# Twelve chunk-1 projection groups moved from the load phase into the segment loop of a recurrent-memory attention kernel, with the whole first V half ahead of the first softmax sums

## Chip, cores, metric

One core of a Trainium2 chip. The metric is the device time of one execution in microseconds (us), as the median of several executions. "Span" is the time from the first to the last instruction in a profiled execution; it is shorter than the device time (858.1 against 859.79 us in before). A ratio of two kernels is the mean time of one kernel's fast runs over the mean of the other's fast runs of the same rounds, so it is not quite the ratio of the medians that are quoted beside it.

Terms: to "evict" is to copy a result out of a PSUM bank, where PE leaves it; "PV" is the product p @ v; "landing" is the moment when a transfer's data have arrived; "issue" as the cause of a wait means that PE waited for nothing that the profile's semaphores show; "residue" is the segment number modulo four.

## The reference, cut to what matters

```python
mem = mem0                                     # 8 memory rows
for s in range(64):                            # 64 segments of 32 rows, one after the other
    h = concatenate([mem, x[32*s : 32*s+32]])  # 40 rows x 512
    q, k, v = h @ Wq, h @ Wk, h @ Wv           # 32 heads of 128
    p = softmax(mask(q @ k.T * scale))
    o = (p @ v) @ Wo
    mem = o[:8]                                # the next segment needs this
    outs.append(o[8:])
h = x + concatenate(outs)
# then a gMLP on layernorm(h): two projections, a 2048x2048 mix, an output projection
```

The memory makes the segments a chain. In the kernel each segment takes the 8 memory rows and the first 24 new rows in the chain itself. The last 8 new rows of each segment ("x rows") are projected apart, for 16 segments (a "chunk") at a time, since they do not depend on the memory.

## The kernel before

One program per engine; the order on PE (TensorE) is what the source says. Three phases: the load phase (16 MB of weights come in, chunk 0 and chunk 1 of the x rows are projected), the loop of 64 segments, and the gMLP tail.

The load phase projects both chunks completely. `start_group` does 16 matmuls into a PSUM bank and evicts it; `load_wo` fetches a quarter of Wo (1 MB); `load_vx(s)` fetches the projected V of the x rows for segment s, which went through DRAM (`vext_d`).

```python
    for n in range(8):                   # V of chunk 0, first half of V of chunk 1
        ...
        start_v(0, n)
        if n % 2 == 1:
            start_v(1, n // 2)
        ...                              # load_wo(0) at n == 4
    load_wo(1)
    for j in range(2):
        load_vx(j)
    for i in range(8, 12):               # K side, both chunks
        for ck in range(2):
            start_group(qkx_mm, qkx_evac, ck, i)
    for n in range(4, 8):                # second half of V of chunk 1
        start_v(1, n)
        if n % 2 == 1:
            load_wo(n // 2)
    for i in range(12, 16):
        for ck in range(2):
            start_group(qkx_mm, qkx_evac, ck, i)
```

Chunks 2 and 3 (48 groups) are projected inside the loop as filler, two quarters of a group ahead of PV and two behind it. One segment in four takes none after segment 12 (`xs = ... if gx and (j4 != 1 or s < 3 * DC)`); other filler (`wq`) is the Wo product of the x rows, eight pieces in four segments.

```python
        S_half(s, 0)                     # scores of heads 0..15
        sm_exp(0)                        # ACT
        for dc in range(3):
            V_half(s, 0, (0, 4), dc)     # three quarters of the first V half
        sm_sums(0)                       # needs the exponential
        sm_ln(0)
        S_half(s, 1)
        sm_exp(1)
        sm_rcp(0)
        V_half(s, 0, (0, 4), 3)
        V_evac(0, "dve")
        V_half(s, 1, (0, 2), 3, 3, 0, held=True)   # held: weights stay, no load
        V_half(s, 1, (2, 4), 3, 3, 1, held=True)
        V_half(s, 1, (0, 2), 2, 3, 0)
        V_half(s, 1, (2, 4), 2, 3, 1, held=True)
        sm_norm(0)
        sm_sums(1)
        ...                              # four more half-width V pieces, evictions
        fill(nw1)
        for f in xs[:2]: f()
        PV_half(s, 0)
        PV_half(s, 1)
        for f in xs[2:4]: f()
        fill(nw2)
        ...                              # eight evictions of PV
        Wo(WOQ, OB, 0, OC)               # needs all four quarters of Wo
        ...
        fill(nw4)
```

The softmax here doesn't subtract the row's maximum and nothing guards it: scores larger than these inputs give would overflow.

Of the kernel before, what the change touches and what calls it, by code (L numbers as in the profile page):

```python
# [178 lines left out]
def fast_path(nc, st, keep, A_x, A_mem0, A_Wq, A_Wk, A_Wv, A_Wo, A_seg_len, B_w_in, B_w_sp, B_b_sp, B_w_out, out):  # L179
# [7 lines left out]
    NSEG = S // SEG  # L187
    RB = S // 128
    DC = D // 128
# [205 lines left out]
    def ln_apply(j):  # L395
        t, tok = xbuf(j)
        k = j % 3
        dve(lambda e: e.tensor_scalar(out=t, in0=t, scalar1=mv1[:, k, 0:1], scalar2=rs1[:, k:k + 1], op0=ALU.subtract, op1=ALU.mult),
            reads=tok + [("mv1", k), ("rs1", k)], writes=tok)
# [102 lines left out]
    def vx_evac(ck, n, bank, eng="act"):  # L502
        if ck == 1 and n < 4:
            t, tok = (hbuf, xo)[n // 2][:, n % 2, :], [(("h", "xo")[n // 2], n % 2)]
        elif ck == 1:
            t = (Vs, V_sb)[n // 2 - 2][:, n % 2, :]
            tok = [("Vs", n % 2)] if n < 6 else [("V", n % 2, g) for g in range(4)]
        elif ck == 0:
            t, tok = part[:, n, :], [("part", n, 0), ("part", n, 1)]
        else:  # L510
            t, tok = Vs[:, 0, :], [("Vs", 0)]
        if eng == "act":
            act(lambda e: e.activation(out=t, in_=ps[:, bank, :], func=ACT.Copy, scale=VSC), reads=[PB(bank)], writes=tok)
        else:
            dve(lambda e: e.tensor_scalar(out=t, in0=ps[:, bank, :], scalar1=VSC, scalar2=None, op0=ALU.mult), reads=[PB(bank)], writes=tok)
        dst = vext_d[ck, n // 4, 2 * (n % 4):2 * (n % 4) + 2, :, :].rearrange("g p f -> p g f")
        sp(lambda e: e.dma_start(dst, t.rearrange("p (g f) -> p g f", g=2)), reads=tok, writes=[("vext", ck, n)])
# [24 lines left out]
    def QK(s, k, dc, first=0, last=3, held=False):  # L542
        b, p0, np_, mi, bank = QKP[k]
        sl = slot(s)
        ws = (w_q, w_k)[mi]
        h0, nh = 16 * b + 2 * p0, 2 * np_
        for c in range(4):
            rhs = ws[:, dc, :].rearrange("p (h c i) -> p c h i", c=4, i=32)[:, c, h0:h0 + nh, :]
            pe(lambda e, c=c, rhs=rhs: mm(e, held, ps[32 * c:32 * c + 32, bank, 0:32 * nh], hT[:, sl, dc, :], rhs,
                                          dc == first, dc == last, (0, 32 * c)),  # L550
               reads=[("hTx", (s // 4) % 3), ("hTm", s, dc // 2), ("W", mi, 2 * b), ("W", mi, 2 * b + 1)], writes=[PB(bank)])
# [60 lines left out]
    def sm_sums(b):  # L612
        bank = UBK[b]
        for c in range(4):
            q = slice(32 * c, 32 * c + 32)
            pe(lambda e, q=q, c=c: e.matmul(ps[q, bank, 224:384], lhsT=ones[:, q], rhs=E_sb[:, b, 0:160], start=True, stop=False,  # L616
                                            skip_group_check=True, tile_position=(0, 32 * c)),
               reads=[("E", b), "ones"], writes=[PB(bank)])
        for c in range(4):
            q = slice(32 * c, 32 * c + 32)  # L620
            pe(lambda e, q=q, c=c: mm(e, True, ps[q, bank, 224:384].rearrange("p (g q) -> p g q", q=40)[:, :, 0:16], ones[:, q],
                                      E_sb[:, b, 160:224].rearrange("p (g q) -> p g q", q=16), False, True, (0, 32 * c)),
               reads=[("Ex", b), "ones"], writes=[PB(bank)])
# [18 lines left out]
    def V_half(s, b, gs, dc, first=0, last=3, held=False):  # L642
        bank = VB[b, gs[0]]
        sl = slot(s)
        w = 128 * (gs[1] - gs[0])
        for c in range(4):
            c0 = (16 * b + 4 * c + gs[0]) * DH
            pe(lambda e, c=c, c0=c0: mm(e, held, ps[32 * c:32 * c + 32, bank, 0:w], hT[:, sl, dc, :], w_v[:, dc, c0:c0 + w],
                                        dc == first, dc == last, (0, 32 * c)),
               reads=[("hTx", (s // 4) % 3), ("hTm", s, dc // 2), ("W", 2, 2 * b), ("W", 2, 2 * b + 1)], writes=[PB(bank)])  # L650

    def V_evac(b, eng, gs=(0, 4)):
        bank = VB[b, gs[0]]
        dst, src = V_sb[:, b, 128 * gs[0]:128 * gs[1]], ps[:, bank, 0:128 * (gs[1] - gs[0])]
        tok = [("V", b, g) for g in range(*gs)]
        if eng == "act":
            act(lambda e: e.activation(out=dst, in_=src, func=ACT.Copy, scale=VSC), reads=[PB(bank)], writes=tok)
        else:
            dve(lambda e: e.tensor_scalar(out=dst, in0=src, scalar1=VSC, scalar2=None, op0=ALU.mult), reads=[PB(bank)], writes=tok)  # L659
# [85 lines left out]
    def load_h(rb):  # L745
        sp(lambda e: e.dma_start(hbuf[:, rb % 2, :], xr[:, rb, :]), writes=[("h", rb % 2)])
# [77 lines left out]
    def load_wo(hq):  # L824
        sp(lambda e, hq=hq: e.dma_start(w_o[:, 8 * hq:8 * hq + 8, :], wor[:, 8 * hq:8 * hq + 8, :]), writes=[("Wo", hq)])
        em.mark_const(("Wo", hq))
# [4 lines left out]
    def start_group(mm, ev, *a):  # L831
        cnt = scnt[0]
        scnt[0] += 1
        bk = ebank[cnt % 4]
        mm(*a, bk)
        ev(*a, bk, "act" if cnt % 2 == 0 else "dve")

    def start_v(ck, n):
        start_group(vx_mm, vx_evac, ck, n)
# [25 lines left out]
    load_wo(1)  # L865
    for j in range(2):
        load_vx(j)
    for i in range(8, 12):
        for ck in range(2):
            start_group(qkx_mm, qkx_evac, ck, i)  # L870
    for n in range(4, 8):
        start_v(1, n)
        if n % 2 == 1:
            load_wo(n // 2)
    for i in range(12, 16):
        for ck in range(2):
            start_group(qkx_mm, qkx_evac, ck, i)


    gx = []  # L880
# [4 lines left out]
    def vx_group(ck, n):  # L885
        gx.append([lambda dc=dc: vx_mm(ck, n, XB, dc) for dc in range(DC)] + [lambda: vx_evac(ck, n, XB, "dve")])

    for ck in (2, 3):
        for n in range(8):
            vx_group(ck, n)  # L890
        for r in range(4):
            for mi in range(2):
                for b in range(2):
                    qkx_group(ck, mi, r, b)

# [18 lines left out]
    for s in range(NSEG):  # L914
        j4 = s % 4
        rb = s // 4
        if j4 == 1 and rb > 0:
            load_h(rb - 1)
        if s == NSEG - 1:
            load_h(rb)  # L920
        if s % 2 == 1 and s // 2 < NWT:
            wT_piece(s // 2)
        if j4 == 0 and 2 <= rb + 2 < RB:
# [6 lines left out]
        if s > 0:  # L930
            mem_out(s - 1, 1)
            for f in late:
                f()
        QK(s, 0, 1)
        QK(s, 1, 1, last=2, held=True)
        QK(s, 0, 2)
# [25 lines left out]
            mask_pe()  # L962
        S_half(s, 0)
        sm_exp(0)
        for dc in range(3):
            V_half(s, 0, (0, 4), dc)
        sm_sums(0)
        sm_ln(0)
        S_half(s, 1)
        lastop["s"] = em.by_eng["pe"][-1]  # L970
        sm_exp(1)
        sm_rcp(0)
        V_half(s, 0, (0, 4), 3)
        V_evac(0, "dve")
        if s == NSEG - 1:
            sp(lambda e: e.dma_start(w_in1, winr[:, :, 0:FH]), writes=["w_in1"], after=[lastop["s"], lastop["x"]])
            sp(lambda e: e.dma_start(bsp_b, bass.AP(B_b_sp.tensor, B_b_sp.offset, [[0, 128], [1, S]])), writes=["bsp"], after=[lastop["k"]])
            for r in range(8, RB - 2):
                xn2T_dma(r, [lastop["s"], lastop["x"]])
        V_half(s, 1, (0, 2), 3, 3, 0, held=True)  # L980
        V_half(s, 1, (2, 4), 3, 3, 1, held=True)
        V_half(s, 1, (0, 2), 2, 3, 0)
        V_half(s, 1, (2, 4), 2, 3, 1, held=True)
        sm_norm(0)
        sm_sums(1)
        sm_ln(1)
        sm_rcp(1)
        V_half(s, 1, (0, 2), 1, 3, 0)
        V_half(s, 1, (0, 2), 0, 3, 0)
        V_half(s, 1, (2, 4), 0, 3, 1, held=True)  # L990
        V_half(s, 1, (2, 4), 1, 3, 1)
        lastop["v"] = em.by_eng["pe"][-1]
        V_evac(1, "dve", (0, 2))
# [4 lines left out]
            lastop["x"] = em.by_eng["pool"][-1]  # L998
            lastop["x"] = em.by_eng["pool"][-1]
        late = []  # L1000
        xs = gx.pop(0) if gx and (j4 != 1 or s < 3 * DC) else []
        if xs:
            nw1, nw2, nw4 = (2 if s < 3 * DC and j4 < 2 else 1), 0, (2 if s < 3 * DC and j4 != 2 else 1)
        else:
            nw1, nw2, nw4 = 3, 2, 1

        def fill(n):
            for f in wq[:n]:
# [37 lines left out]
            late.append(lambda: ln_stats(7))  # L1046
        if s == 3:
            late.append(lambda: (ln_apply(7), x_flip(7, RB, hTe[:, 0, :, :], [("hTe", 0, 0), ("hTe", 0, 1)])))
        if j4 == 1 and rb >= 2:
            late.append(lambda rb=rb: (xn2_apply(rb - 2, rb % 2), xn2_store(rb - 2, rb % 2)))  # L1050
        if j4 == 1 and rb > 0:
            assert not wq
            late.append(lambda rb=rb: WoX_evac(rb - 1))
            wq.append(lambda rb=rb: F_group(rb - 1, WXB))
            wq.append(lambda rb=rb: WoX_scatter(rb - 1, WXB))
            nw4 = 0
        if j4 == 2 and rb > 0:
            late.append(lambda rb=rb: F_add(rb - 1, WXB))
        if j4 == 3 and rb > 0:
            late.append(lambda rb=rb: h_done(rb - 1))  # L1060
        if s + 1 < NSEG:
            if j4 == 3:
                assert not wq
                wq.extend(lambda rb=rb, k=k: WoX_mm(rb, k // 2, range(4 * (k % 2), 4 * (k % 2) + 4)) for k in range(8))
            fill(nw4)
            assert not wq or j4 != 2
        else:
            for f in late:
                f()
        if s + 2 < NSEG:  # L1070
# [964 lines left out]
```

## Time and profile before

| | before |
|---|---|
| median of three runs | 861.03 us (859.86 to 861.23) |
| span of the profiled run | 858.1 us |
| granted TensorE clock | 1.0 |
| first exponential (loop has begun 4 us before) | 56.85 us |
| segments 1 to 11, mean | 9.91 us |
| segments 12 to 62, mean | 9.75 us |
| after the last first-half exponential | 183.8 us |

Segments are measured from one start of the first-half exponential on ACT to the next; the segment numbers in this text are those. From the page of before: busy time by engine, and the chain of work that ended last.

```profile
span 858.1 us, 45452 instructions
PE 844.5 (98%) x22504; PEld 426.0 (50%) x18920; DVE 506.2 (59%) x1312; ACT 471.3 (55%) x1359; POOL 156.1 (18%) x423
...
PE 94%; DMA 3%; DVE 1%; SPq 1%; issue 0%; ACT 0%
```

PE is the bound, but "98% busy" is not "98% at work", as this trace shows. The timeline of before in a middle segment, where the columns are start, duration, engine, line, instruction and operands:

```profile
254.52 0.82 PE L289 MATMUL f_ps<-f_arena,f_hT 128*32 128x512 bf16 x12
255.35 0.25 PE L616 MATMUL f_ps<-f_E_sb,f_ones 128*32 128x160 bf16 x4
...
256.83 0.39 PE L752 MATMUL f_ps<-f_arena,f_cTx 128*32 128x512 bf16 x4
257.04 0.60 PE L289 MATMUL f_ps<-f_arena,f_hTe 128*32 128x512 bf16 x8
257.58 0.20 PE L667 MATMUL f_ps<-f_E_sb,f_V_sb 32*128 32x40 bf16 x4
```

Four column-tiled 128x512 matmuls ("one quad") take 0.217 us (by their starts, nine in 1.95 us from 52.79 us on). Twelve take 0.65; but the first sums (L616) start 0.83 us after the twelve V matmuls began: 0.18 us of stall that no busy figure shows. The same before PV (L667): 0.54 us for two quads, which take 0.43.

Segment 0 of before:

```profile
59.48 0.27 PE L290 MATMUL f_ps<-f_arena,f_hT 128*32 128x256 bf16 x1 [0.69 <-issue]
...
61.10 0.51 PE L702 MATMUL f_ps<-f_arena,f_cT 128*32 128x256 bf16 x11
61.99 1.48 PE L702 MATMUL f_ps<-f_arena,f_cT 128*32 128x256 bf16 x45 [0.37 <-DMA f_arena<-in_A_Wo_dram]
```

What to see: the Wo product (L702) of segment 0 is stopped after 11 of its matmuls until the last quarter of Wo has landed (61.94 us in the landing records). So already before the change, Wo came just in time, though the loop began at 52.8 us.

### The profile page before, as it was taken

To read this page: it belongs to the slowest core of one execution; us is meant where nothing else is said; L and a number is where in the kernel's file an instruction comes from. 1 tells how busy PE (TensorE), PEld (TensorE's weight loads), DVE (VectorE), ACT (ScalarE), POOL (GpSimd) and SP (SyncE) were. 2 spreads that over 40 slices of the span, in tenths; PEclk is the share of its full clock that TensorE was granted. 3 is DMA by queue.
4 is the path that set the end of the run, shared out by engine and by line. 5 is a ranking of instruction groups with operands and counts; after the bars stand their busy time and mean duration, and the time that the engine had idled before them with its cause. 6 is when DMAs were issued, how large, how long until landed. Compare 5 with 4: busy or idle time off the path is not lost.

```text
span 858.1 us, 45452 instructions
## 1 busy us (share of the span) xinstructions
PE 844.5 (98%) x22504; PEld 426.0 (50%) x18920; DVE 506.2 (59%) x1312; ACT 471.3 (55%) x1359; POOL 156.1 (18%) x423
## 2 busy tenths in 40 slices
PE   8999999999999999999999999999999999999997
PEld 8664545444444544454444444444444444444443
DVE  3546666666666666666666666666665554453443
ACT  3446666666666666666666666666666655400000
POOL 0712112121112112121211212121111132100000
PEclk9999999999999999999999999999999999999999
DMA  9982222224141221222241413343121690032101
GB/s 315 365 256 68 72 76 70 66 40 86 31 87 41 70 46 51 72 68 60 71 86 38 80 43 94 69 83 71 47 69 43 193 277 1 1 111 98 38 13 41
DMA packets 114713, 75.25 MB, mean 88 GB/s; under 512 B 70728, under 2 KB 100560, under 8 KB 114512
## 3 DMA queue, kind: packets, MB, share of 16 engines
q1 hardware_dynamic: 114224, 72.06, 30.7%
q8 instruction: 164, 2.69, 1.3%
q14 instruction: 37, 0.30, 0.1%
q10 hardware_dynamic: 288, 0.20, 0.1%
HBM read 39.46 MB, written 20.58 MB: 70 GB/s over the span
## 4 chain that ended last, share of the span: by engine, by line
PE 94%; DMA 3%; DVE 1%; SPq 1%; issue 0%; ACT 0%
PE f_ps L289 30%; PE f_ps L702 13%; PE f_ps L290 13%; PE f_ps L1150 11%; PE f_ps L752 3%; PE f_ps L498 3%; PE f_ps L1224 3%; PE f_ps L667 3%; PE f_ps L1112 3%; PE f_ps L616 3%; PE f_ps L1143 3%; PE f_ps L463 2%; PE f_ps L596 1%; DMA f_arena<-in_A_Wq_dram 1%; DMA f_arena<-in_A_Wo_dram 1%; PE f_ps L673 1%
## 5 line engine op out<-in xcount | busy, mean ns | idle before, releaser
L289 PE MATMUL f_ps<-f_arena,f_hT 128*32 128x512 bf16 (+1 forms) x5120 | 352.4, 337 | 1.1
L290 PE MATMUL f_ps<-f_arena,f_hT 128*32 128x256 bf16 (+1 forms) x3072 | 214.0, 308 | 0.7 <-issue 0.7
L289 PEld LDWEIGHTS f_ps<-f_arena,f_hT 128*32 128x32 bf16 x5120 | 120.0, 96 | 170.0 <-issue 86.7
L560 ACT ACTIVATE f_Tst<-f_ps 128x512 bf16<-128x512 f32 (+1 forms) x320 | 149.7, 509 | 56.9 <-PE f_ps L289 53.3
L702 PE MATMUL f_ps<-f_arena,f_cT 128*32 128x256 bf16 x4096 | 130.4, 274 | 1.9 <-ACT f_cT L687 1.1
L639 POOL TENSOR_TENSOR f_E_sb<-f_R_sb,f_E_sb 128x64 bf16<-128x64 f32 x128 | 47.8, 374 | 373.1 <-ACT f_R_sb L631 373.1
L568 DVE STREAM_TRANSPOSE f_QT<-f_Tst 128x256 uint32<-128x256 uint32 x128 | 57.1, 446 | 94.5 <-ACT f_Tst L560 94.5
L702 PEld LDWEIGHTS f_ps<-f_arena,f_cT 128*32 128x32 bf16 x4096 | 89.9, 94 | 36.0 <-ACT f_cT L687 23.1
L1150 PE MATMUL f_ps<-f_arena 128*128 128x512 bf16 x448 | 100.6, 379 | 0.0
L659 DVE TENSOR_SCALAR f_V_sb<-f_ps 128x512 bf16<-128x512 f32 (+1 forms) x128 | 70.5, 551 | 41.5 <-PE f_ps L289 41.0
L689 DVE TENSOR_SCALAR f_cT<-f_ps 128x160 bf16<-128x160 f32 x256 | 65.0, 316 | 36.0 <-PE f_ps L673 36.0
L714 ACT ACTIVATE f_part<-f_ps 128x256 bf16<-128x256 f32 x128 | 49.0, 383 | 59.8 <-PE f_ps L702 56.8
L687 ACT ACTIVATE f_cT<-f_ps 128x160 bf16<-128x160 f32 x256 | 57.1, 310 | 36.8 <-PE f_ps L673 36.8
L1150 PEld LDWEIGHTS f_ps<-f_arena 128*128 128x128 bf16 x448 | 43.7, 98 | 52.8
L568 DVE STREAM_TRANSPOSE f_KT<-f_Tst 128x128 uint32<-128x128 uint32 (+1 forms) x192 | 65.9, 356 | 2.8
L627 ACT ACTIVATE f_R_sb<-f_ps 128x160 f32<-128x160 f32 x128 | 38.8, 304 | 33.7 <-PE f_ps L290 33.7
L1156 DVE TENSOR_TENSOR f_arena<-f_ps,f_arena 128x512 f32<-128x512 f32 x28 | 19.3, 689 | 54.4 <-PE f_ps L1150 52.4
L609 ACT ACTIVATE f_E_sb<-f_ps 128x224 bf16<-128x224 f32 x128 | 45.9, 359 | 0.0
L635 DVE TENSOR_TENSOR f_E_sb<-f_R_sb,f_E_sb 128x160 bf16<-128x160 f32 x128 | 44.7, 349 | 0.0
L631 ACT ACTIVATE f_R_sb<-f_R_sb 128x160 f32<-128x160 f32 x128 | 42.5, 332 | 2.0
L752 PE MATMUL f_ps<-f_arena,f_cTx 128*32 128x512 bf16 x512 | 40.6, 380 | 0.0
L289 PE MATMUL f_ps<-f_arena,f_hTe 128*32 128x512 bf16 x512 | 39.1, 382 | 0.0
(119 smaller groups left out, 1022.3 us busy)
## 6 DMA issues: line engine op xcount, KB each, us to landing
wT_d<-f_wst SPq DMA_DIRECT2D x32, 256.0 KB, 3.7
f_arena<-wT_d SPq DMA_DIRECT2D x32, 256.0 KB, 4.7
f_arena<-in_A_Wv_dram SPq DMA_DIRECT2D x4, 1024.0 KB
f_arena<-in_A_Wk_dram SPq DMA_DIRECT2D x4, 1024.0 KB, 16.1
f_arena<-in_A_Wo_dram SPq DMA_DIRECT2D x4, 1024.0 KB
f_Vx<-vext_d SPq DMA_DIRECT2D x128, 32.0 KB
f_arena<-in_A_Wq_dram SPq DMA_DIRECT2D x3, 1024.0 KB
vext_d<-f_Vs SPq DMA_DIRECT2D x18, 128.0 KB
```

Source lines behind the costliest of these rows:

```text
L289: return e.matmul(out, lhsT=lhsT, rhs=rhs, start=start, stop=stop, skip_group_check=True, tile_position=pos)
L290: return e.add_instruction(mybir.InstMatmult(name=nc.get_next_instruction_name(), engine=mybir.EngineType.PE, ins=[e.lower_ap(rhs), e.lowe ...
L560: act(lambda e: e.activation(out=st_.rearrange("p (hp i r) -> p hp i r", i=32, r=2), in_=ps[:, bank, 0:64 * np_].rearrange("p (hp r i) -> ...
L568: dve(lambda e: e.transpose(out=dst, in_=src), reads=tok, writes=[(nm, b, k) for k in halves(b, p0, np_)])
L639: pool(lambda e: e.tensor_tensor(out=ev, in0=rv, in1=ev, op=ALU.mult), reads=[("R", b), ("Ex", b)], writes=[("Ex", b)])
L659: dve(lambda e: e.tensor_scalar(out=dst, in0=src, scalar1=VSC, scalar2=None, op0=ALU.mult), reads=[PB(bank)], writes=tok)
L687: act(lambda e: e.activation(out=dst, in_=src, func=ACT.Copy, scale=UNSC), reads=[PB(PVB[c])], writes=tok)
L689: dve(lambda e: e.tensor_scalar(out=dst, in0=src, scalar1=UNSC, scalar2=None, op0=ALU.mult), reads=[PB(PVB[c])], writes=tok)
L702: pe(lambda e, h=h, g=g, i=i, b=b, c=c: e.matmul(ps[32 * g:32 * g + 32, bank, 0:d1 - d0], lhsT=cTh[:, i, 8:40], rhs=w_o[:, h, d0:d1], star ...
L714: act(lambda e: e.activation(out=part[:, s % 8, d0:d1], in_=ps[:, bank, 0:d1 - d0], func=ACT.Copy), reads=[PB(bank)], writes=[("part", s % ...
L752: pe(lambda e, h=h, g=g, i=8 * qr + bg: e.matmul(ps[32 * g:32 * g + 32, WXB, :], lhsT=cTx[:, rb % 2, i, :], rhs=w_o[:, h, :], start=(i < 4 ...
L1150: pe(lambda e: e.matmul(ps[:, bank, 0:TB], lhsT=z2[:, sc, fb * 128:(fb + 1) * 128], rhs=wTb[tb % 2][:, :, sc, :], start=(sc == 0), stop=(s ...
```

## The change

The intent: take 12 of the 24 chunk-1 groups out of the load phase (four V groups, eight K-side groups), so that the loop begins earlier, and do one group in each of segments 0 to 59, where PE has stalls to fill; put the whole first V half ahead of the first sums, into the stall seen above; spread the Wo pieces of the x rows evenly. The core of the diff (the shifts of `h_done`, `xn2_apply`, `F_add` by one segment and the last segment's special cases are cut):

```diff
     load_wo(1)
     for j in range(2):
         load_vx(j)
-    for i in range(8, 12):
-        for ck in range(2):
-            start_group(qkx_mm, qkx_evac, ck, i)
-    for n in range(4, 8):
-        start_v(1, n)
-        if n % 2 == 1:
-            load_wo(n // 2)
-    for i in range(12, 16):
-        for ck in range(2):
-            start_group(qkx_mm, qkx_evac, ck, i)
+    for i in range(8, 16):
+        start_group(qkx_mm, qkx_evac, 0, i)
+        if i in (11, 13):
+            load_wo(i // 2 - 3)
...
-    for ck in (2, 3):
-        for n in range(8):
+    for ck in range(1, 4):
+        for n in range(4 if ck == 1 else 0, 8):
             vx_group(ck, n)
         for r in range(4):
-            for mi in range(2):
+            for mi in range(1 if ck == 1 else 0, 2):
...
-        for dc in range(3):
+        for dc in range(DC):
             V_half(s, 0, (0, 4), dc)
+        V_evac(0, "dve")
         sm_sums(0)
         sm_ln(0)
         S_half(s, 1)
         sm_exp(1)
         sm_rcp(0)
-        V_half(s, 0, (0, 4), 3)
-        V_evac(0, "dve")
...
-        V_half(s, 1, (0, 2), 3, 3, 0, held=True)
-        V_half(s, 1, (2, 4), 3, 3, 1, held=True)
+        V_half(s, 1, (0, 2), 3, 3, 0)
+        V_half(s, 1, (2, 4), 3, 3, 0, held=True)
         V_half(s, 1, (0, 2), 2, 3, 0)
-        V_half(s, 1, (2, 4), 2, 3, 1, held=True)
+        V_half(s, 1, (2, 4), 2, 3, 0, held=True)
+        V_half(s, 1, (0, 2), 1, 3, 0)
+        V_half(s, 1, (0, 2), 0, 3, 0)
         sm_norm(0)
         sm_sums(1)
         sm_ln(1)
         sm_rcp(1)
-        V_half(s, 1, (0, 2), 1, 3, 0)
-        V_half(s, 1, (0, 2), 0, 3, 0)
-        V_half(s, 1, (2, 4), 0, 3, 1, held=True)
+        V_half(s, 1, (2, 4), 0, 3, 1)
         V_half(s, 1, (2, 4), 1, 3, 1)
...
-        xs = gx.pop(0) if gx and (j4 != 1 or s < 3 * DC) else []
+        xs = gx.pop(0) if gx else []
+        if j4 == 0 and rb > 0:
+            wq.extend(... WoX_mm(rb - 1, ...) ...)
+        nw1, nw2, nw4 = (2, 1, 2, 1)[j4], 0, 1
...
```

More of the change, by code (lines that the diff above doesn't have):

```diff
@@ L504, in vx_evac @@
             t, tok = (hbuf, xo)[n // 2][:, n % 2, :], [(("h", "xo")[n // 2], n % 2)]
-        elif ck == 1:
-            t = (Vs, V_sb)[n // 2 - 2][:, n % 2, :]
-            tok = [("Vs", n % 2)] if n < 6 else [("V", n % 2, g) for g in range(4)]
         elif ck == 0:
@@ L918, in fast_path @@
             load_h(rb - 1)
-        if s == NSEG - 1:
-            load_h(rb)
         if s % 2 == 1 and s // 2 < NWT:
@@ L933, in fast_path @@
                 f()
+        if s == NSEG - 1:
+            load_h(rb)
         QK(s, 0, 1)
@@ L1000, in fast_path @@
         late = []
-        xs = gx.pop(0) if gx and (j4 != 1 or s < 3 * DC) else []
-        if xs:
-            nw1, nw2, nw4 = (2 if s < 3 * DC and j4 < 2 else 1), 0, (2 if s < 3 * DC and j4 != 2 else 1)
-        else:
-            nw1, nw2, nw4 = 3, 2, 1
+        xs = gx.pop(0) if gx else []
+        if j4 == 0 and rb > 0:
+            assert not wq
+            wq.extend(lambda rb=rb, k=k: WoX_mm(rb - 1, k // 2, range(4 * (k % 2), 4 * (k % 2) + 4)) for k in range(8))
+        nw1, nw2, nw4 = (2, 1, 2, 1)[j4], 0, 1
+        if not xs:
+            nw1, nw2 = 1, nw1 - 1
         def fill(n):
@@ L1048, in fast_path @@
             late.append(lambda: (ln_apply(7), x_flip(7, RB, hTe[:, 0, :, :], [("hTe", 0, 0), ("hTe", 0, 1)])))
+        fill(nw4)
         if j4 == 1 and rb >= 2:
+            late.append(lambda rb=rb: h_done(rb - 2))
+        if j4 == 2 and rb >= 2:
             late.append(lambda rb=rb: (xn2_apply(rb - 2, rb % 2), xn2_store(rb - 2, rb % 2)))
-        if j4 == 1 and rb > 0:
+        if j4 == 2 and rb > 0:
             assert not wq
@@ L1055, in fast_path @@
             wq.append(lambda rb=rb: WoX_scatter(rb - 1, WXB))
-            nw4 = 0
-        if j4 == 2 and rb > 0:
+        if j4 == 3 and rb > 0:
+            assert not wq
             late.append(lambda rb=rb: F_add(rb - 1, WXB))
-        if j4 == 3 and rb > 0:
+        if s + 1 == NSEG:
             late.append(lambda rb=rb: h_done(rb - 1))
-        if s + 1 < NSEG:
-            if j4 == 3:
-                assert not wq
-                wq.extend(lambda rb=rb, k=k: WoX_mm(rb, k // 2, range(4 * (k % 2), 4 * (k % 2) + 4)) for k in range(8))
-            fill(nw4)
-            assert not wq or j4 != 2
-        else:
             for f in late:
```

## The prediction

> **What bounds it now.** The chain of waits is 94% PE, and the page has PE busy 98% at granted clock 1.0, but "busy" hides stalls. I measured segments of the loop between the starts of successive first-half exponentials on ACT. Segments 12 to 62 take 9.75 us each, segments 1 to 11 take 9.91. Call four column-tiled 128x512 matmuls one quad (0.217 us). The timeline by matmul starts shows where a segment (20 and 21, say) still stalls: 0.19 us before the first sums (they wait for the exponential), 0.10 us before the first PV matmuls (they wait for the V eviction and the normalisation chain), about 0.13 us inside PV, 0.07 us before Wo. Filler in those places is nearly free: segments with 5 quads of filler take 9.71 us, with 6 9.75, with 8 10.13. The loop is at the knee between latency and PE work.
>
> In the load phase DMA is saturated (99%, about 385 GB/s) until 40 us, PE works without waiting, and the loop begins at 52.8. Segment 0 already waits for the last quarter of Wo (landed 61.9, the 0.37 us wait that the timeline shows).
>
> **What the change does.**
> - Load phase: 4 V groups (64 matmuls, 3.64 us) and 8 K-side groups (128 matmuls of 128x128, 7.32 us) go: 10.96 us of PE. The K groups now need the last Wk quarter at 40.2; it lands at 40.9, so about 0.7 us of wait. The loop should start near 42.8.
> - But Wo cannot come as much earlier. Its last two quarters are now issued near 49.7 and 50.2 instead of 51.2 and 52.9, behind the Vx loads, with four 128 KB stores fewer between. At 2.7 us per MB (the spacing of the weight landings) the last lands near 57.5. Wo of segment 0 would begin near 51, so PE idles about 6 us there. The load phase therefore gains about 4.4 us, not 10.
> - [...]here the clock record falls 3.9 us after the last matmul.[...]
> - Loop: 12 groups x 4 quads, 10.4 us of PE, come in, filling segments that had none: 26 quads per four segments throughout (before: 26 early, 22 later).
> - The whole first V half before the first sums puts a quad into the 0.19 us stall; the chain sums, ln, reciprocal, normalise, PV moves only about 0.03 us later, so one more quad fits before PV free. I expect 9.76 us per segment everywhere: segments 1 to 11 gain 0.15 each (1.7 us), 12 to 62 lose about 0.01 each. ACT and DVE have room (55 to 60%).
> - The last segments and the gMLP tail (183.8 us after the last exponential) stay.
>
> **Sum.** -4.4 (load)[...] -1.1 (loop): about -4.5 us, 856.5 us; 8 in 10 between 852.5 and 861. Faster by over 2%: 2%. Within 2%: 96%. Slower: 2%.
>
> **What would show it.** First exponential near 47 us instead of 56.8; a PE wait of 5 to 7 us in segment 0 on the Wo load; last Wo quarter near 57.5; first exponential of segment 1 near 64 to 66 instead of 68; segments 9.72 to 9.80 us in every residue of four; no 0.19 us stall before the first sums; a dip of the granted clock near 55 to 62 us or none; tail unchanged.
>
> **What would make it wrong.** Wo landing earlier or later than 57.5;[...] the extra evictions on ACT/DVE in every segment delaying the part or memory evictions (0.1 us per segment is 6 us); or the V-first order shortening the chain to PV, in which case the loop gains up to 0.1 us per segment.

Where the text is cut, it said that the wait for Wo might lower PE's clock, allowed 1.2 us for that, and named 2 us for a longer fall; no trace or run had shown these, and both figures were the author's estimate. One term of the sum is cut with them: it read -4.4 (load) +1.2 (clock) -1.1 (loop), which makes -4.3 us, put as about -4.5 us and 856.5 us. The 3.9 us that stand there are from the end of before: its last matmul ends at 853.36 us, and the clock record falls to 0.5 at 857.22.

## The result

| | before | after |
|---|---|---|
| median | 861.13 us (859.86 to 862.25, 4 runs) | 861.31 us (860.37 to 862.40, 4 runs) |
| ratio | | 1.0003, 95% interval 0.9982 to 1.0024 |
| span of the profiled run | 858.1 us | 860.6 us |

No difference. The predicted 856.5 us was 0.6% too low and the range (to 861.0) just missed. From the page of after, the same lines as shown of before:

```profile
span 860.6 us, 45965 instructions
PE 837.9 (97%) x22497; PEld 440.7 (51%) x19432; DVE 513.7 (60%) x1318; ACT 471.1 (55%) x1361; POOL 165.2 (19%) x423
...
PE 94%; DMA 2%; SPq 1%; DVE 1%; ACT 1%; issue 1%
```

There are 512 PE weight loads more (19432 against 18920): the new V order gives up two re-uses of loaded weights in each segment, eight loads. A middle segment of after, at the places shown of before:

```profile
253.95 1.03 PE L289 MATMUL f_ps<-f_arena,f_hT 128*32 128x512 bf16 x16
254.81 0.24 PE L613 MATMUL f_ps<-f_E_sb,f_ones 128*32 128x160 bf16 x4
...
256.06 0.60 PE L749 MATMUL f_ps<-f_arena,f_cTx 128*32 128x512 bf16 x8
256.49 0.60 PE L289 MATMUL f_ps<-f_arena,f_hTe 128*32 128x512 bf16 x8
257.02 0.27 PE L664 MATMUL f_ps<-f_E_sb,f_V_sb 32*128 32x40 bf16 x16
```

Four quads of V (x16) now stand before the sums and take 0.86 us, so there is no stall there; and four quads of filler before PV instead of three. The segment is no longer for that. That half of the change did what it was meant to do. Segment 0 of after:

```profile
50.27 0.19 PE L664 MATMUL f_ps<-f_E_sb,f_V_sb 32*128 32x40 bf16 x1 [1.19 <-DMA f_Vx<-vext_d]
...
52.25 0.59 PE L498 MATMUL f_ps<-f_arena,f_hTe 128*32 128x512 bf16 x1 [0.69 <-issue]
52.26 0.80 PE L699 MATMUL f_ps<-f_arena,f_cT 128*32 128x256 bf16 x7
56.27 0.41 PE L699 MATMUL f_ps<-f_arena,f_cT 128*32 128x256 bf16 x4 [3.21 <-DMA f_arena<-in_A_Wo_dram]
60.39 2.74 PE L699 MATMUL f_ps<-f_arena,f_cT 128*32 128x256 bf16 x45 [3.71 <-DMA f_arena<-in_A_Wo_dram]
```

PE gets to Wo nearly nine microseconds earlier (52.26 us instead of 61.10) and stands there for 7 us. When it goes on, the 45 remaining matmuls take 2.74 us where before took 1.48: the clock is at half (the clock records show 0.5 from 52.12 to 65.77 us). Both facts in one view, busy time by stretch (segment 0; 1 to 11; 12 to 62; the rest); the columns are the stretch, its length, the engines' busy times, granted clock, DMA share and GB/s. First before, then after:

```profile
56.85:68.02 11.17, 10.10 (x328) 4.98 (x268) 6.58 (x19) 6.10 (x20) 2.19 (x6) 1.00 0.58 159
68.02:177.07 109.05, 108.61 (x3616) 53.80 (x2992) 70.52 (x197) 70.25 (x216) 20.95 (x54) 1.00 0.28 70
177.07:674.24 497.17, 494.26 (x16596) 242.74 (x13736) 319.22 (x897) 332.07 (x1012) 96.98 (x250) 1.00 0.27 62
674.24:858.10 183.86, 177.85 (x1040) 82.68 (x1008) 85.30 (x159) 39.57 (x76) 17.67 (x39) 1.00 0.28 88
```

```profile
46.39:68.63 22.24, 13.21 (x328) 6.29 (x276) 6.76 (x19) 6.11 (x20) 2.47 (x6) 0.69 0.73 197
68.63:175.84 107.21, 106.37 (x3604) 55.59 (x3072) 70.08 (x194) 72.21 (x221) 21.71 (x52) 1.00 0.23 57
175.84:676.25 500.41, 497.34 (x16788) 262.26 (x14336) 330.30 (x910) 333.98 (x1016) 104.92 (x252) 1.00 0.28 65
676.25:860.60 184.35, 177.87 (x1041) 83.33 (x1024) 86.32 (x160) 39.68 (x76) 17.81 (x39) 1.00 0.29 88
```

The loop begins 10.5 us earlier, and segment 0 lasts 11.1 us longer. Segments 1 to 11 gain 1.8 us; segments 12 to 62, where a loss of 0.5 us was expected, lose 3.2. Single executions scatter (859.86 to 862.25 us for the same kernel), so before and after were traced again later; all traces, in us:

| stretch | before, three traces | after, two traces | difference of means |
|---|---|---|---|
| to the first exponential | 56.85, 56.21, 56.16 | 46.39, 47.05 | -9.7 |
| segment 0 | 11.18, 11.10, 10.71 | 22.24, 19.93 | +10.1 |
| segments 1 to 11 | 109.05, 108.99, 109.00 | 107.20, 107.46 | -1.7 |
| segments 12 to 62 | 497.17, 498.22, 498.32 | 500.41, 499.90 | +2.3 |
| the rest | 183.83, 184.05, 183.98 | 184.35, 183.74 | +0.1 |

A warning on the last column: the traced executions of before took 859.8, 860.4 and 859.9 us, all among its faster ones (the medians of its rounds are 860.4 to 861.8), those of after 862.4 and 859.8. The differences add up to +1.1 us, while the ratio of all fast runs says +0.3. So up to about a microsecond of the column can be the choice of executions.

The clock needs a second look too. In after it fell to half at 52.12 us, before PE's first wait for Wo (53.06 us). From 48.78 us, where its first PV matmuls began, to the fall PE had stood 1.19 and 0.22 us for Vx and most of 0.69 us for "issue". So the wait for Wo did not bring the clock down; what the trace shows ahead of the fall are these shorter waits. That they brought it down is not shown: the trace of experiment 2 has 0.99 us for Vx and 0.91 us for "issue" at the same place and no half clock. Full clock came back at 65.77 us, 5.4 us after PE had gone on with Wo (60.39).

So three questions: what holds segment 0, is the loop worth anything, and what are the 2.3 us.

### The profile page after: what moved, and what is told of

Read it like the earlier page. It is cut to its first block, busy times and chain, and to the rows that moved or that the text cites. A ratio compares the mean times of both kernels' runs of the same rounds, so it can differ in the third digit from the quotient of the medians.

```text
span 860.6 us, 45965 instructions
## 1 busy us (share of the span) xinstructions
PE 837.9 (97%) x22497; PEld 440.7 (51%) x19432; DVE 513.7 (60%) x1318; ACT 471.1 (55%) x1361; POOL 165.2 (19%) x423
## 4 chain that ended last, share of the span: by engine, by line
PE 94%; DMA 2%; SPq 1%; DVE 1%; ACT 1%; issue 1%
PE f_ps L289 32%; PE f_ps L699 14%; PE f_ps L290 12%; PE f_ps L1138 11%; PE f_ps L498 3%; PE f_ps L749 3%; PE f_ps L664 3%; PE f_ps L1212 3%; PE f_ps L1100 3%; PE f_ps L1131 3%; PE f_ps L463 2%; PE f_ps L593 1%; PE f_ps L613 1%; DMA f_arena<-in_A_Wo_dram 1%; PE f_ps L670 1%; PE f_ps L720 1%
## 5 line engine op out<-in xcount | busy, mean ns | idle before, releaser
L289 PE MATMUL f_ps<-f_arena,f_hT 128*32 128x512 bf16 (+1 forms) x5632 | 361.0, 332 | 0.2
L289 PEld LDWEIGHTS f_ps<-f_arena,f_hT 128*32 128x32 bf16 x5632 | 134.7, 96 | 160.9 <-issue 69.5
L290 PE MATMUL f_ps<-f_arena,f_hT 128*32 128x512 bf16 (+1 forms) x2560 | 190.1, 316 | 0.0
L699 PE MATMUL f_ps<-f_arena,f_cT 128*32 128x256 bf16 x4096 | 133.2, 276 | 8.5 <-DMA f_arena<-in_A_Wo_dram 6.9
L636 POOL TENSOR_TENSOR f_E_sb<-f_R_sb,f_E_sb 128x64 bf16<-128x64 f32 x128 | 56.9, 445 | 353.1 <-ACT f_R_sb L628 353.1
L711 ACT ACTIVATE f_part<-f_ps 128x256 bf16<-128x256 f32 x128 | 49.0, 383 | 66.5 <-PE f_ps L699 62.4
L656 DVE TENSOR_SCALAR f_V_sb<-f_ps 128x512 bf16<-128x512 f32 (+1 forms) x128 | 71.0, 555 | 13.7 <-PE f_ps L289 13.7
L632 DVE TENSOR_TENSOR f_E_sb<-f_R_sb,f_E_sb 128x160 bf16<-128x160 f32 x128 | 41.7, 326 | 23.3 <-ACT f_R_sb L628 23.3
L289 PE MATMUL f_ps<-f_arena,f_hTe 128*32 128x512 bf16 x640 | 48.9, 382 | 0.0
L749 PE MATMUL f_ps<-f_arena,f_cTx 128*32 128x512 bf16 x512 | 44.0, 379 | 0.0
```

Of the source, the lines that this page charges most:

```text
L289: return e.matmul(out, lhsT=lhsT, rhs=rhs, start=start, stop=stop, skip_group_check=True, tile_position=pos)
L290: return e.add_instruction(mybir.InstMatmult(name=nc.get_next_instruction_name(), engine=mybir.EngineType.PE, ins=[e.lower_ap(rhs), e.lowe ...
L636: pool(lambda e: e.tensor_tensor(out=ev, in0=rv, in1=ev, op=ALU.mult), reads=[("R", b), ("Ex", b)], writes=[("Ex", b)])
L656: dve(lambda e: e.tensor_scalar(out=dst, in0=src, scalar1=VSC, scalar2=None, op0=ALU.mult), reads=[PB(bank)], writes=tok)
L699: pe(lambda e, h=h, g=g, i=i, b=b, c=c: e.matmul(ps[32 * g:32 * g + 32, bank, 0:d1 - d0], lhsT=cTh[:, i, 8:40], rhs=w_o[:, h, d0:d1], star ...
L711: act(lambda e: e.activation(out=part[:, s % 8, d0:d1], in_=ps[:, bank, 0:d1 - d0], func=ACT.Copy), reads=[PB(bank)], writes=[("part", s % ...
```

## The experiments

Each result is given as the ratio to before of the same rounds. "Half clock" is the stretch in which the clock records of the trace show 0.5. "Excess" is the sum, over the segments 12 to 62 that are longer than 9.8 us, of what each has over 9.75 us.

### 1. The old load phase with the new loop

```diff
-    for i in range(8, 16):
-        start_group(qkx_mm, qkx_evac, 0, i)
-        ...
+    # the load phase of before
+    gx.extend([] for _ in range(12))     # segments 0 to 11 take no group
-    for ck in range(1, 4): ...
+    for ck in (2, 3): ...
```

> The load phase of before (all twelve groups in it), the loop of after. Theory A (the loop is held by latency at about 9.73 us a segment whatever filler is in it, and the gain of the load phase was lost to the Wo wait in segment 0): first exponential at 56.8 us and segment 0 at 11.2 us as before, segments 1 to 62 at 9.72 to 9.75 us, about 857 to 859.5 us in all, 2 to 4 us under after. Rival B (the loop of after is what cost the gain, because its rearrangement or its extra work is slower): 861 us or more, segments 1 to 11 not under 9.9.

Measured: 861.75 us, ratio 1.0015 (0.9997 to 1.0032). In the trace segment 0 is as before (11.4 us) and segments 1 to 11 take 107.1 us (-2), as theory A said; but 12 to 62 take 499.4 us (+1.5 against the mean of before), and the total is not better. The floor is confirmed: the medians by residue of four are 9.79, 9.72, 9.74, 9.72 with a group in each of segments 12 to 59. The total that A gave is a miss, by the stretch 12 to 62.

### 2. PE kept busy while it waits for Wo

```diff
+        if s == 0:
+            for _ in range(36):          # nobody reads this bank in segment 0
+                pe(lambda e: e.matmul(ps[:, WXB, :], lhsT=onesrc[:, 0:128], rhs=w_o[:, 0, :], ...))
         Wo(WOQ, OB, 0, OC)
```

> After, with 36 128x512 matmuls (7.8 us) in segment 0 ahead of Wo, into a bank that nobody reads, so that PE is busy while it waits for Wo. Theory A1 (the granted clock fell to half in that idle time and cost about 2.2 us after Wo came): no stretch at half clock, first exponential of segment 1 near 66.4 instead of 68.6, about 2 us under after. Rival (the half clock costs nothing, only the landing of Wo counts): same as after within 0.5 us. If the added matmuls delay Wo: slower.

Measured: no half clock, and the first exponential of segment 1 at 66.60 us, as A1 said (after: 68.64, and 66.98 in its second trace, whose half clock was 10.2 us long instead of 13.7). Counted from the first Wo matmul after the wait, which leaves the landing out, it is 6.2 us (60.42 to 66.60), against 8.2 and 7.4 in the two traces of after. But the total is 860.12 us, ratio 1.0001 (0.9983 to 1.0020), which the interval does not tell from after's. The cost of the half clock is seen in segment 0 (2.74 us for 45 matmuls against 1.48); a gain in the total is not shown.

### 3. Segment 0 without the need for three quarters of Wo

Wrong arithmetic on purpose: in segment 0 all heads take their weights from the first quarter. (The comparison with the reference still passed its tolerance.)

```diff
-                h = 16 * b + 4 * c + g
+                h = (16 * b + 4 * c + g) % hm          # hm = 8 in segment 0, else 32
```

> Wrong result on purpose: in segment 0 the Wo matmuls take all weights from the first quarter of Wo, so that segment 0 waits for no other quarter. Theory A (the whole gain of the load phase sits behind the Wo landing): segment 0 lasts about 12 us instead of 22.2 (what stays is a wait of about 1.4 us for Vx), segment 1 may wait a little for the other quarters, no half clock; 850 to 853 us. Rival B (PE work only moved, the loop gives it back): 859 or more.

Measured: 855.87 us, ratio 0.9944 (0.9931 to 0.9956): 4.8 us under before, about half of what A expected. Rival B is out: the moved groups are not paid back in full in the loop (segments 1 to 62 take 608.2 us, against 606.9 in the mean of before). But segment 0 still took 16.3 us, not 12. Its waits on PE:

```profile
PE f_ps L498 <- issue: 2.3, 1, 2.3
PE f_ps L664 <- DMA f_Vx<-vext_d: 1.3, 2, 0.8
...
```

So not all was behind Wo. There are waits for Vx, and one of 2.3 us for "issue", a wait for nothing that semaphores show; the half clock came again (6.8 us, from 51.63 us on), here without any wait for Wo. What that "issue" is, the last three experiments ask.

### 4. Eight K groups stay, four V groups move

```diff
     for i in range(8, 16):
-        start_group(qkx_mm, qkx_evac, 0, i)
+        for ck in range(2):
+            start_group(qkx_mm, qkx_evac, ck, i)
```

> The eight K groups (7.3 us of PE) stay in the load phase, only the four V groups move; loop of after. Theory A: loop begins near 49.6 us, PE waits 1 to 3 us for Wo in segment 0, no half clock, first exponential of segment 1 at 65 to 66.5, about 857 to 859 us. Rival B (every group moved off the load phase gains or costs by itself): between e1 and after in proportion to the groups moved.

Measured: 859.59 us, ratio 0.9985 (0.9970 to 0.9999). Rival B is not borne out, since the ratio lies under those of both experiment 1 and after, though the intervals overlap. But A is a miss too. PE stopped for "issue" twice (0.87 us until 54.2, 2.11 us until 60.4), the second time past the landing of Wo (59.73), so no wait for Wo shows; the half clock came for 3.4 us, and the first exponential of segment 1 was at 68.1: outside A's 65 to 66.5, as the total is outside its 857 to 859.

### 5. Transfers in another order

```diff
+    load_wo(0); load_wo(1)              # right behind Wk
     ...                                 # eight chunk-0 V stores
-    load_wo(1); load_vx(0); load_vx(1)  # with chunk-1 stores between, load_wo(2), (3) later
+    load_wo(2); load_vx(0); load_wo(3); load_vx(1)
+    for f in stores1: f()               # the four chunk-1 V stores last
     # and K groups i = 12..15 of chunk 1 stay in the load phase
```

> After, with the transfers in another order (first half of Wo right behind Wk, the chunk-0 V stores, the third quarter, Vx of segment 0, the last quarter; the chunk-1 stores last) and four K groups (3.7 us) left in the load phase. Theory A (what the change gains is limited by the landing of Wo and Vx, which wait behind other transfers and behind stores to land): last quarter of Wo near 55.5 us instead of 60.3, first exponential of segment 1 at 61 to 63 instead of 68.6, no or a short half clock, 4 to 7 us under before. Rival (DMA bandwidth alone sets it, the order does not matter): the last quarter still lands at 59 to 61, same as before within 2 us.

Measured: 859.14 us, ratio 0.9974 (0.9960 to 0.9989). The last quarter landed at 57.45 us (after: 60.34), the first exponential of segment 1 came at 64.8, and PE still waited 2.8 us for Wo, with a half clock of 3.4 us. Direction as A said, size less: both times are two microseconds later than A's, and the gain is 2.2 us (0.26% of 861) instead of 4 to 7. The order moves the landing, so the rival is out. The gain in the total is that of the order and of the four kept groups together.

### 6. The second V half in pairs

The eight weight loads that the change added are saved again, with the same matmuls.

```diff
-        V_half(s, 1, (0, 2), 0, 3, 0)
+        V_half(s, 1, (2, 4), 1, 3, 0, held=True)
         ...                             # second sums
-        V_half(s, 1, (2, 4), 0, 3, 1)
-        V_half(s, 1, (2, 4), 1, 3, 1)
+        V_half(s, 1, (0, 2), 0, 3, 0)
+        V_half(s, 1, (2, 4), 0, 3, 0, held=True)
```

> After, with the second V half in pairs that use one weight load for both matmuls, before and after the second sums: 8 weight loads fewer in a segment, as many as before had, same matmuls. Theory F (PE's stalls in segments 12 to 62 that fall every 256 PE instructions are waits for the instruction fetch, and the 8 more instructions of a segment make them longer): the excess of segments over 9.8 us falls from 3.7 to about 1 us as in before, about 2 us under after. Rival (the stalls are chance or come from DVE and ACT): same as after within 0.5 us, excess 2 us or more.

The places that theory F names are seen in the trace of after: its long "issue" waits in segments 12 to 62 stand at PE instructions 12737, 27329 and 32961, multiples of 256 apart, and the queue that its page calls "instruction" brought 166 packets of 16,384 bytes for 41,929 PE records. That the waits are for these packets is the theory.

Measured: 860.72 us, ratio 0.9985 (0.9970 to 0.9999), but the excess of segments 12 to 62 over 9.8 us did not fall (4.6 us; the traced execution was the slowest of the six). Theory F in this form, that these eight loads make the excess, fell.

### 7. Before with those eight loads added

```diff
-        V_half(s, 1, (0, 2), 3, 3, 0, held=True)
+        V_half(s, 1, (0, 2), 3, 3, 0)
-        V_half(s, 1, (2, 4), 0, 3, 1, held=True)
+        V_half(s, 1, (2, 4), 0, 3, 1)
```

> Before, with 8 weight loads more in a segment (the two re-uses that the change undoes), nothing else. Theory F (instruction fetch): excess of segments 12 to 62 over 9.8 us rises from 0.8 to 2 to 3.5 us, about 2 us slower than before. Rival (the loads are hidden behind matmuls and cost nothing): same as before within 0.5 us.

Measured: 862.35 us, ratio 1.0001 (0.9985 to 1.0016): the total does not show the 2 us. The trace does: segments 12 to 62 take 500.3 us and their excess is 3.6 us, as F said. Experiments 6 and 7 together were inconclusive, which is why 12 to 14 were made.

### 8. After with the old V order

```diff
-        for dc in range(DC):
+        for dc in range(3):
             V_half(s, 0, (0, 4), dc)
         ...                             # the V block of before
```

> After, with the V order of before (three quarters of the first V half ahead of the first sums). Theory A (V first puts one quad into a 0.19 us stall): with four quads of filler ahead of PV, segments with residue 0 and 2 take about 9.85 to 9.9 us, those with 1 and 3 stay at 9.72 to 9.75; about 3.5 us more in the loop, less about 2 us if theory F holds, since it has 8 weight loads fewer. Rival (the V order does nothing): all residues 9.72 to 9.78.

Measured: 865.17 us, ratio 1.0037 (1.0021 to 1.0054). The segment medians by residue are 9.97, 9.73, 9.95, 9.75: the two residues with four quads before PV are longer by 0.2 us, the others are not. The stall before the sums is back, and the matmuls after it run 0.2 us later up to PV:

```profile
254.97 0.82 PE L289 MATMUL f_ps<-f_arena,f_hT 128*32 128x512 bf16 x12
255.80 0.25 PE L613 MATMUL f_ps<-f_E_sb,f_ones 128*32 128x160 bf16 x4
```

V first is what lets the loop take four more quads in four segments with no longer segment medians. It is worth about 3 us here (ratio 1.0037 without it, 1.0003 and 1.0005 with it).

### 9. Before and after again

> Before again, unchanged, for a second trace. If the excess of segments 12 to 62 over 9.8 us (0.8 in the first trace, which was one of the fastest executions; 1.9 to 4.6 in all other kernels' traces) is chance of an execution, this trace shows 2 to 4 us; if it belongs to before, under 1.5 again. First exponential of segment 1 at 68, segments 1 to 11 at 109 in any case.

Measured: 861.98 us of two runs; segments 12 to 62 at 498.2 us, excess 1.9 us, between the two outcomes that were named (under 1.5, or 2 to 4).

> After again, unchanged, on the same chip as the next two: within 0.2% of before; first exponential of segment 1 near 68.5, 13.7 us of half clock.

Measured: 860.80 us, ratio 1.0005 (0.9990 to 1.0020). The first exponential of segment 1 came at 66.98 us, half clock 10.2 us: less than the first trace, from an earlier landing of Wo (59.57 us) and an earlier return of the clock.

### 10. Four K groups kept, last Wo quarter ahead of all Vx loads, paired V

Experiment 5 with `load_wo(2); load_wo(3); load_vx(0); load_vx(1)` and the order of experiment 6.

> The earlier Wo order with four K groups kept (as e5), the last Wo quarter now ahead of all Vx loads, and the paired second V half. Theory A: last quarter near 56.4 instead of 57.5, first exponential of segment 1 at 62.5 to 64, 3 to 5 us under before. Rival (order exhausted): as e5, 0.26% under before.

Measured: 856.94 us, ratio 0.9953 (0.9937 to 0.9969). The last quarter landed at 56.54 as expected, but the first exponential of segment 1 came only at 65.4: PE stood 3.7 us at PV until Vx had landed (56.78), just after Wo, and the half clock came for 3.4 us. The wait had changed its name. The total is in A's range.

### 11. The same with all eight K groups kept

Only the four V groups move into the loop.

> The same with all eight K groups kept, only the four V groups moved: PE arrives at Wo after it has landed. Theory A: no wait for Wo in segment 0, no half clock, first exponential of segment 1 at 63 to 64.5, 3 to 4.5 us under before. Rival (something else in the load phase holds it[...]): first exponential of segment 1 at 66 or later, under 0.3% below before.

Measured: 855.52 us, ratio 0.9938 (0.9921 to 0.9955), 5.2 us under before, a little more than A's 3 to 4.5: the best version, and correct. Segment 0 takes 10.36 us at full clock and the first exponential of segment 1 is at 62.93 us. What is left on PE in segment 0, and the stretch itself:

```profile
PE f_ps L708 <- issue: 0.2, 1, 0.2
```

```profile
52.57:62.93 10.36, 9.91 (x328) 5.19 (x268) 6.66 (x19) 6.12 (x20) 2.48 (x6) 1.00 0.62 166
```

Why Wo comes earlier shows in the DMA view from 40 to 62 us (slices of 0.55 us): GB/s of after, then of this kernel.

```profile
GB/s 302 236 318 339 306 317 363 351 347 333 252 214 250 339 384 387 375 217 82 84 64 152 114 264 382 387 387 361 335 356 354 346 358 341 304 169 49 30 128 118
```

```profile
GB/s 350 356 348 369 335 342 348 362 348 339 325 322 226 239 278 285 348 372 335 331 369 365 367 367 320 284 326 311 212 87 239 21 0 124 130 63 54 46 196 272
```

In after the queues run dry near 50 to 53 us (64 to 152 GB/s), because the queue's own engine stands at the Vx loads until the V stores that they read have landed (48.5 us in the landing records), and issues the last two quarters of Wo only at 50.4 and 50.9. Before has such a hole too, less deep (129 to 155 GB/s from 52.1 to 53.8 us). The queue's own timeline, first of after, then of this kernel:

```profile
45.35 5.00 SPq L520 DMA_DIRECT2D f_Vx<-vext_d  x4
50.39 1.09 SPq L822 DMA_DIRECT2D f_arena<-in_A_Wo_dram  x2
```

```profile
45.63 2.27 SPq L831 DMA_DIRECT2D f_arena<-in_A_Wo_dram  x2
48.08 3.20 SPq L529 DMA_DIRECT2D f_Vx<-vext_d  x4
```

With Wo ahead of the Vx loads there is no such hole (331 to 369 GB/s in the slices from 50 to 53 us). The last quarter is issued 4.7 us earlier than in after and lands at 54.9 us, 5.4 us earlier. The whole gain lies there: the first exponential of segment 1 comes 4.5 us earlier than in the mean of before (62.93 against 67.40), while segments 1 to 62 take 607.1 us against 606.9.

This version contains the order of transfers, the eight kept groups and the paired V. That 4, 5 and 6 alone gave 0.9985, 0.9974 and 0.9985 says that no one of them is the whole; they were not taken apart further, and 10 and 11 overlap in their intervals. Nor was the new order of transfers put into before with nothing moved; how much of the gain needs the four moved groups is not known.

### 12 to 14. What the "issue" stalls are

In all traces the long "issue" waits of PE (over 0.2 us) stand at the same place: where the count of PE instructions (matmuls and weight loads), divided by 256, leaves 193 (192 in the loop of experiment 2, whose trace lacks one record). In the first trace of before they stand at instructions 1985 and 21953, in after at 1729, 12737, 27329 and 32961. In every case a 16,384-byte packet of the queue that the page calls "instruction" had ended 1.2 to 1.7 us before PE went on. At the other boundaries of this kind, where PE did not wait, that packet had ended 2.0 to 2.6 us before in the median of each trace, and never less than 1.1. In the three longest waits (2.30 us in experiment 3, 2.11 in 4, 2.08 in the second trace of after) the packet began only when PE stood at the boundary or at most three instructions before it; in the median it began about 200 to 210 instructions before. There is one such packet to 256 PE instructions: 164 for 41,424 PE records in the first trace of before, 166 for 41,929 in after. At most boundaries PE does not wait (of about 160 in a trace of before, two show a wait over 0.15 us, and in all traces 0 to 9); where it does, it stalls 0.2 to 0.9 us in the loop and up to 2.3 us in segment 0 (experiment 3). To size these stalls, I took for each matmul of a segment the median interval from the one before it, over segments 12 to 61 of the same kind, and summed what single intervals exceed it by over 60 ns, at those block boundaries.

> Before, with all twelve weight re-uses of a segment's Q, K and V matmuls undone: 48 weight loads more in a segment (8 in the earlier run), the same matmuls in the same order. Theory F2 (PE gets its instructions in packets of 256, stalls where a packet comes late, and the stalls grow with the number of PE instructions in a segment): the excess at every 256th PE instruction in segments 12 to 61, 0.9 and 1.7 us in the two traces of before and 3.6 in the one with 8 loads more, is over 6 us, and the kernel at least 0.6% slower than before. Rival (the stalls are chance of an execution): 1 to 4 us there; a slower kernel would then show the time elsewhere, spread over all segments alike.

Edit: all twelve `held=True` of the Q, K and V matmuls of before removed. Measured: 867.85 us, ratio 1.0095 (1.0070 to 1.0119); the boundary stalls are 5.8 us (F2 asked for over 6, a near miss, and the rival for 1 to 4), while three of the four segment medians hardly move (9.76, 9.73, 9.76); that of residue 3 is 9.87 instead of 9.71, which is 2 us in all. Segments 12 to 62 take 504.2 us. The waits of PE there are nearly all "issue":

```profile
PE f_ps L702 <- issue: 1.3, 2, 0.8
PE f_ps L667 <- issue: 1.0, 2, 0.7
PE f_ps L723 <- issue: 0.5, 2, 0.3
PE f_ps L702 <- ACT f_cT L687: 0.4, 1, 0.4
...
```

> The kernel with 8 loads more again, for a second trace. Theory F2: 2.5 to 4.5 us at every 256th PE instruction. Rival: anything from 0.9 to 4.

Measured: 2.75 us at the boundaries (the earlier trace 3.6); one run, 862.02 us.

> Before a third time, for its trace. Theory F2: 0.7 to 2 us at every 256th PE instruction. Rival: anything from 0.9 to 4.

Measured: 1.9 us at the boundaries; one run, 859.89 us. All traces together:

| kernel | boundary stalls in segments 12 to 61, us |
|---|---|
| before, three traces | 0.9, 1.7, 1.9 |
| before with 8 weight loads more per segment, two traces | 3.6, 2.75 |
| before with 48 more | 5.8 |
| after, two traces | 3.1, 2.2 |
| the other kernels with the new loop and a group in segments 12 to 59 (1 to 6, 10, 11) | 2.2 to 4.4 |

The size depends on which segments are taken as one kind. A second reckoning, by residue alone, gives 1.0, 2.2 and 2.3 for before, 3.8 and 3.2 with 8 loads more, 8.2 with 48 more, and 4.0 and 3.3 for after. So in the loop of before, more PE instructions per segment go with longer stalls. In the new loop the eight loads do not show: its seven traces with them (after twice, experiments 1 to 5) have 2.1 to 4.3 us, 3.4 in the mean, and its four without them (6, 8, 10, 11) 2.1 to 5.2, 3.6 in the mean.

The new loop has more of them in that stretch for two reasons: 8 weight loads per segment, and 12 groups (32 instructions each) more between segments 12 and 59, since the chunk-1 groups take the places of segments 0 to 11. That experiment 6, which removes only the loads, did not bring the excess back to before's fits this, but does not show it. How the two parts share it is not settled, nor why some packets come late: chance of an execution is as large as the effect of 8 loads.

## Why the prediction was wrong

Point by point:

- **"Segment 0 already waits for the last quarter of Wo", so the load phase gains less than it saves: right.** The loop began 9.7 us earlier and segment 0 took 10.1 us longer.
- **"At 2.7 us per MB (the spacing of the weight landings) the last lands near 57.5": the step that failed.** The wait and its place were right; the time from the issue to the landing of the last quarter was put too short. Landing was at 60.34 and 59.57 us. The issue did not make the difference: it was at 50.89 in the first trace and in the second at 50.24, as predicted ("near 49.7 and 50.2"). The prediction allowed 7.3 us from there, and the runs took 9.5 and 9.3. Before itself had taken 9.0 (52.92 to 61.94), so its trace already spoke against 7.3. 2.7 us per MB is a rate of about 388 GB/s, read from the stretch to 40 us, in which the DMA engines were busy throughout (90% or more in every slice from 10 to 40 us of before, 380 GB/s in the mean); between issue and landing the DMA of after moved 275 and 283 GB/s in the mean, and 2.6 million bytes, of which the two quarters are 2.1. Cost against the prediction: about 2.5 us (mean landing 59.96 against 57.5).
- **The 1.2 us that were allowed for the clock (an estimate, cut above): half clock came, but not from the wait for Wo, and it cost more.** In the first trace of after the clock fell at 52.12 us, before PE's first wait for Wo (53.06 us) and after shorter waits for Vx and "issue" (1.19, 0.22 and most of 0.69 us; experiment 3 shows 6.8 us of half clock without any wait for Wo). What brought it down is not shown. From the landing to the first exponential of segment 1 there were 8.3 and 7.4 us; in the first trace of before 6.1 (68.02 less 61.94). So it cost 1.3 to 2.2 us.
- **"9.76 us per segment everywhere" as the floor: right but for one value.** Medians by residue in segments 12 to 59 are 9.77, 9.73, 9.89 and 9.73 in the first trace of after, 9.77, 9.72, 9.76 and 9.73 in the second; the 9.89 is outside the 9.72 to 9.80 that the prediction named. Segments 1 to 11 gained 1.7 us (predicted 1.7), and experiment 8 shows that this hangs on V first.
- **"12 to 62 lose about 0.01 each": failed.** They lost 2.3 us in the traces instead of 0.5, of which up to about one can be the choice of executions. I costed 12 groups by PE time alone and not by the PE instructions that they add (31,124 matmuls and weight loads in segments 12 to 62 of after, 30,332 in before, with the 8 loads more in each segment); the runs show stalls at places 256 PE instructions apart (1.5 us in the mean of three traces of before, 2.65 in the two of after, 5.8 in before with 48 loads more). That they account for about 1.1 us of the loss is an estimate, the difference of the means 2.65 and 1.5. Of the rest I can name no cause that the runs separate.
- **"The tail stays": right** (183.95 against 184.05 us in the means).

The sum: predicted -4.5 us, of which about 2.5 went to Wo, 0.6 to the half clock beyond what was allowed, and 1.8 to the stretch 12 to 62. That makes +0.4; the medians say +0.2, the means of the traces' spans +1.1.

## What to carry to other kernels

Here work taken out of a phase that a transfer bounds turned into a wait for that transfer (9.7 us saved before the loop, 10.1 us more in segment 0), so move the transfers first: the change alone gave nothing, and with Wo issued ahead of loads that wait for stores, eight of the twelve groups left where they hid the transfer, and paired V loads, it gave 0.6%. The rate read while the DMA engines were busy throughout (2.7 us per MB, 388 GB/s) was not the rate past the point where the issuing engine had to wait (275 and 283 GB/s); the issue-to-landing time of the same transfer in the trace of before (9.0 us) would have been the better estimate. And filler adds PE instructions beside its PE time: the stalls at places 256 PE instructions apart came to 0.9 to 1.9 us in before and 2.2 to 3.1 in after. That more instructions lengthen them is here argued from means that chance blurs, and shown clearly only for 48 loads more per segment (5.8 us).
